# h stays in PSUM through h·cos(h): whole turns written as integers, no SBUF copy of h

## The chip, the cores and the metric

One Trainium2 chip, of which one core is used. The metric is device time in microseconds, the median of several executions. Of the kernel before three runs are known: 733.02, 732.50 and 732.21 us, median 732.5 us.

## The reference, cut to what matters

Attention over 2 batches of 8 heads and 768 positions gives `x`, 1536 tokens by 512. Two feed-forward parts follow. The change lies in the first of them:

```python
h = x @ w_in            # 1536x512 @ 512x2048
g = h * np.cos(h)
x = g @ w_out           # 2048x512
...
a = x @ w_a             # 512x1536
b = x @ w_b
return (a * b @ w_out2)
```

## The kernel before, in words

**Products.** Each float32 factor is split into a high part (rounded to the matrix engine's format `F32R`) and a low part (the rest), and a product takes three matmuls: high by high, high by low, low by high (lines 411 to 413, 473 to 475, 501 to 503). The 1536 tokens are three chunks `c` of 512. The first part's 2048 hidden columns are 16 blocks of 128, in groups of 4, 6 and 6. For a block and a chunk, `h_step` makes an `h` of 128x512 in PSUM with 12 matmuls, `h_mid` turns it into g, and `split_g` into the pair `gh` (ScalarE, line 455) and `gl` (GpSimd's subtraction, line 138). There are 48 such `h`, numbered 0 to 47 here in the order in which they are made. When all blocks of a group have their g for a chunk, `y_part` runs four partial products `y`, each of three matmuls for every block of the group, and VectorE adds them up in SBUF (lines 477, 479).

**Steps of h_mid.** ScalarE copies h/2π from PSUM into the SBUF tile `hs` (line 434). VectorE adds 0.25 and a large constant, which rounds to whole turns (line 435), then subtracts the constant and `hs` (line 436). ScalarE takes the sine (line 440), which by the shift of a quarter turn is the cosine of h. VectorE multiplies `hs` times 2π with it (line 443). Both `hs` and `u` have three buffers; a buffer of `u` is free again once GpSimd has made `gl` from it. Blocks 0 and 1 of the first chunk are made while the attention ends, by `early_turns` and `early_rest`, which call `h_turns`, `h_sin` and `h_mult` one by one; the other 46 go through `h_mid`.

**Weights.** A weight comes as a float64 in memory. Each of 68 blocks is converted: ScalarE takes an absolute value (line 351), VectorE runs four operations on whole numbers and bounds (lines 358 to 362), ScalarE rounds the high part (line 368), GpSimd subtracts for the low part (line 138). `fetch` writes these conversions between the products, up to 20 blocks ahead. The load of the next block waits on SyncE's queue until VectorE's last operation on the block two before has read its buffer.

**Buffers in PSUM.** In this part the tag `h` has four buffers of one bank, used in turn by `h` and, in the second part, by `a` and `b`; `y` and `o` have four more. A buffer of `h` is released by the last instruction that reads it.

**Order.** In the first and second feed-forward part only TensorE's instructions stand in the written order (`LATE_ORDER`). The orders on VectorE, ScalarE and GpSimd are made by a planner from modelled times when the kernel is built; on the chip each engine then runs its list strictly in that order. `in_turn` keeps the sines in the order in which they are written.

Of the kernel before, what the change touches and what calls it, by code (L numbers as in the profile page):

```python
# [10 lines left out]
F32 = mybir.dt.float32  # L11
# [3 lines left out]
I32 = mybir.dt.int32  # L15
AF = mybir.ActivationFunctionType
ALU = mybir.AluOpType
# [6 lines left out]
TWO_PI = 2.0 * math.pi  # L24
# [4 lines left out]
SC, TR = 2, 4  # L29
QP = (3, 13)  # L30
PTB = 3
# When each step of a tile's attention is due, in tiles from the tile's own; the steps are written in the order of these.
TABLE = {'S0': -0.894, 'T3': 0.134, 'TX': 1.203, 'TQ': -1.895, 'P0': 0.161, 'TK': -1.643, 'S1': -0.525, 'P1': 0.341, 'T0': -0.22, 'T1': -0.233, 'P2': 0.506, 'P3': 0.588, 'T2': -0.085, 'RL': 0.846, 'FIN': 0.963, 'L2': 0.298, 'B0': -0.757, 'B1': -0.676, 'L3': 0.443, 'XL': 1.457, 'B2': -0.371, 'B3': -0.219, 'KL': -1.201, 'L0': 0.036, 'L1': -0.108, 'H2': 0.02, 'H3': 0.339, 'XH': 1.381, 'E0': -0.666, 'E1': -0.347, 'QH': -1.59, 'KH': -1.325, 'E2': -0.243, 'H0': -0.146, 'H1': -0.218, 'E3': -0.066, 'SQ': -2.793, 'V': -0.869, 'PK': -0.368, 'QL': -1.371, 'FK': -1.121, 'VG': 1.106, 'LQ': -4.408, 'LK': -2.688, 'LV': -1.259}
BIAS = (-2.925, 0.022)
CONV = ((-0.4, 0.192), (0, 1.145), (2, 1), (11.427, 0.333))
# [12 lines left out]
def tile_kernel(ctx, tc, q, k, v, n_global, n_local, w_in, w_out, w_a, w_b, w_out2, out):  # L48
    nc = tc.nc
# [17 lines left out]
    mo = ctx.enter_context(tc.tile_pool(name="mo", bufs=2))  # L67
# [4 lines left out]
    def f(ap):  # L72
        return ap.bitcast(F32)
# [11 lines left out]
    ng, nl = counts[:, 0, 3:4], counts[:, 1, 3:4]  # L85

    def read_counts():
        """The two int64 scalars as floats: high word (one more where the low word reads as negative) times 2^32, plus the low word."""
        w = counts
        nc.vector.tensor_copy(out=w[:, :, 0:2], in_=words)  # L90
        nc.vector.tensor_scalar(out=w[:, :, 2:3], in0=w[:, :, 0:1], scalar1=0.0, scalar2=None, op0=ALU.is_lt)
        nc.vector.tensor_tensor(out=w[:, :, 2:3], in0=w[:, :, 2:3], in1=w[:, :, 1:2], op=ALU.add)
        nc.vector.scalar_tensor_tensor(out=w[:, :, 3:4], in0=w[:, :, 2:3], scalar=4294967296.0, in1=w[:, :, 0:1], op0=ALU.mult, op1=ALU.add)
# [19 lines left out]
    quarter = const.tile([P, 1], F32, tag="quarter", name="quarter")  # L113
# [33 lines left out]
    pinned = [True]  # L147

    def in_turn(x):
        """Keeps the functions that share no table of ScalarE in the order in which they are written."""  # L150
        if prev and pinned[0]:
            tc.add_manual_dep(x.ins, prev[0], mybir.DependencyInfo(mybir.DependencyClass.NoSync, mybir.DependencyReason.DATA),
                              reason="table order")
        prev[:] = [x.ins.name]
# [36 lines left out]
        nc.vector.tensor_tensor(out=kx[:, i % 2, 1, hps], in0=tk, in1=f(kx[:, i % 2, 0, hps]), op=ALU.subtract)  # L191

    def first_keys(i):
        """Keeps the first keys of a batch when its first tile has come."""
        if i % NQ == 0:
            pool_copy(kg, f(kx[:, i % 2, :, :, :GLOB]).rearrange("p a h s -> p (a h) s"))

    def put_first_keys(i):
        """After the scores of tile i, the first keys of the batch take the place of its own first ones."""
        if 0 < i % NQ < NQ - 1:  # L200
            pool_copy(kx[:, i % 2, :, :, :GLOB].rearrange("p a h s -> p (a h) s"), f(kg))

    def split_v(i):
        """Three bfloat16 parts of V, the first with a column of ones beside it for the sum of the weights."""
        b, t = divmod(i, NQ)
        vx = at.tile([P, H, 3 * D + 2], BF16, tag="vx", name=f"vx{i}", bufs=3)
        vn = nat.pop(i)["v"]
        nc.gpsimd.memset(vx[:, :, D:D + 2], 1.0)
        pool_copy(vx[:, :, 0:D], vn)
        pool_sub(vn, vn, vx[:, :, 0:D])  # L210
        pool_copy(vx[:, :, VP[1]], vn)
        pool_sub(vx[:, :, VP[2]], vn, vx[:, :, VP[1]])
        if t == 0:
            vg = at.tile([GLOB, H, 3 * D + 2], BF16, tag="vg", name=f"vg{i}", bufs=1)
            pool_copy(vg, vx[:GLOB])
            vg_of[b] = vg
        vx_of[i] = vx
# [77 lines left out]
        x_of[i] = xn  # L295

    def first_values(i):
        """After the products of tile i with V, the first values of the batch take the place of its own first ones."""
        if 0 < i % NQ < NQ - 1:
            nc.sync.dma_start(out=vx_of[i][:GLOB], in_=vg_of[i // NQ])  # L300

# [81 lines left out]
    now_conv = {}  # L383

    def conv_op(x):
        """The next of VectorE's four operations on block x."""
        if x not in now_conv:
            now_conv[x] = conv_ops(x)
        now_conv[x].pop(0)()
        if not now_conv[x]:  # L390
            del now_conv[x]
            done[1] += 1
# [38 lines left out]
    def h_turns(hps, shape, nm):  # L431
        hs = mo.tile(shape, F32, tag="hs", name="hs" + nm, bufs=3)
        u = mo.tile(shape, F32, tag="u", name="u" + nm, bufs=3)
        nc.scalar.activation(out=hs, in_=hps, func=AF.Copy, scale=1.0 / TWO_PI)  # L434
        nc.vector.tensor_scalar(out=u, in0=hs, scalar1=0.25, scalar2=MAGIC, op0=ALU.add, op1=ALU.add)  # L435
        nc.vector.scalar_tensor_tensor(out=u, in0=u, scalar=MAGIC, in1=hs, op0=ALU.subtract, op1=ALU.subtract)  # L436
        return hs, u

    def h_sin(hs, u):
        in_turn(nc.scalar.activation(out=u, in_=u, func=AF.Sin, bias=quarter, scale=-TWO_PI))  # L440

    def h_mult(hs, u):
        nc.vector.scalar_tensor_tensor(out=u, in0=hs, scalar=TWO_PI, in1=u, op0=ALU.mult, op1=ALU.mult)

    def h_mid(hps, shape, nm):
        x = h_turns(hps, shape, nm)
        h_sin(*x)
        h_mult(*x)
        return split_g(x[1], shape, nm)

    def split_g(u, shape, nm):
        pool, bufs = (post["mo"], NG[1]) if slot("g", *NG) else (mo, NG[0])
        gh = pool.tile(shape, F32R, tag="gh", name="gh" + nm, bufs=bufs)
        gl = pool.tile(shape, F32R, tag="gl", name="gl" + nm, bufs=bufs)
        nc.scalar.activation(out=gh, in_=u, func=AF.Copy)  # L455
        pool_sub(gl, u, f(gh))
        return gh, gl
# [114 lines left out]
            fn()  # L572

    def general_attention(ga, gps):
        """Any n_global and n_local: every key, with the masks worked out for each tile of queries."""
        xT_of.clear()
        half = S // 2
        for b in range(B):
# [10 lines left out]
            for t in range(NQ):  # L589
# [27 lines left out]
                for h in range(H):  # L617
# [5 lines left out]
                    for z in range(2):  # L623
# [3 lines left out]
                                                       op0=ALU.mult, op1=ALU.add)  # L627
# [18 lines left out]
                i = b * NQ + t  # L646
                c, u = divmod(i, TPC)
# [41 lines left out]
            nc.scalar.activation(out=d[:, 0, x], in_=d[:, 1, 1 - x], func=AF.Copy)  # L689

    def early_h(j, half):
        """A product of the second part while the attention's last steps are on their way."""
        if half == 0:
            early[0, j] = psum("h", [P, CH], f"h0_0_{j}")
        proj(early[0, j], ready[j], xT_of[0], range(2 * half, 2 * half + 2))
# [11 lines left out]
    other_i = const.tile([P, 1], I32, tag="otheri", name="other_i")  # L707

    def beyond():
        """Whether n_global and n_local go beyond what the tiles above hold."""  # L710
        nc.vector.tensor_scalar(out=other[:, 0:1], in0=nl, scalar1=1.0, scalar2=None, op0=ALU.is_lt)
        nc.vector.tensor_scalar(out=other[:, 1:2], in0=nl, scalar1=float(P - GLOB + 1), scalar2=None, op0=ALU.is_gt)
        nc.vector.tensor_scalar(out=other[:, 2:3], in0=ng, scalar1=float(GLOB), scalar2=None, op0=ALU.is_gt)
        nc.vector.tensor_tensor(out=other[:, 3:4], in0=other[:, 0:1], in1=other[:, 1:2], op=ALU.add)
        nc.vector.tensor_tensor(out=other[:, 3:4], in0=other[:, 3:4], in1=other[:, 2:3], op=ALU.add)
        nc.vector.tensor_copy(out=other_i, in_=other[:, 3:4])
# [3 lines left out]
    def boxed(x, fn):  # L720
# [4 lines left out]
    step = {  # L725
        "LQ": lambda i: i and load("q", i),
        "LK": lambda i: i and load("k", i),
        "LV": lambda i: load("v", i),
        "SQ": scale_q, "V": split_v,
        "TQ": boxed("Q", lambda i: turned("q", i)), "QH": lambda i: q_hi(i, box["Q", i]), "QL": lambda i: q_lo(i, box.pop(("Q", i))),  # L730
        "TK": boxed("K", lambda i: turned("k", i)), "KH": lambda i: k_hi(i, box["K", i]), "KL": lambda i: k_lo(i, box.pop(("K", i))),
        "FK": first_keys, "PK": put_first_keys, "RL": weights_sum, "FIN": finish, "VG": first_values,
        "TX": boxed("X", turn_x), "XH": lambda i: x_hi(i, box["X", i]), "XL": lambda i: x_lo(i, box.pop(("X", i)))}
    for quad in range(2):
        step[f"S{quad}"] = boxed(quad, lambda i, quad=quad: scores(i, quad))
        for a in range(2):
            x = 2 * quad + a
# [6 lines left out]
    parts = slice(0, HP // 2), slice(HP // 2, HP)  # L744
# [68 lines left out]
```

## Time and profile before

| what | value |
|---|---|
| median of three runs | 732.5 us |
| span of the profiled execution, first to last instruction | 731.0 us |
| around the span (median less span) | 1.5 us |
| PE busy / VectorE (DVE) busy / ScalarE (ACT) busy / GpSimd (POOL) busy | 676.8 / 510.7 / 303.3 / 289.8 us |
| mean granted TensorE clock | 0.967 of full speed |
| chain that ended last | PE 50%, DVE 35%, ACT 6% |

The page gives no time of its own for the profiled execution beside its span. Busy times are summed over the whole span; the attention takes about the first 119 us, the first feed-forward part lies between some 114 and 450 us, the second behind it. A row `a <- b` in the lists of waits reads: a sat idle until b had ended.

### The profile page before, as it was taken

To read this page: it belongs to the slowest core of one execution; us is meant where nothing else is said; L and a number is where in the kernel's file an instruction comes from. 1 tells how busy PE (TensorE), PEld (TensorE's weight loads), DVE (VectorE), ACT (ScalarE), POOL (GpSimd) and SP (SyncE) were. 2 spreads that over 40 slices of the span, in tenths; PEclk is the share of its full clock that TensorE was granted. 3 is DMA by queue.
4 is the path that set the end of the run, shared out by engine and by line. 5 is a ranking of instruction groups with operands and counts; after the bars stand their busy time and mean duration, and the time that the engine had idled before them with its cause. 6 is when DMAs were issued, how large, how long until landed. Compare 5 with 4: busy or idle time off the path is not lost.

```text
span 731.0 us, 10359 instructions
## 1 busy us (share of the span) xinstructions
PE 676.8 (93%) x3936; PEld 556.5 (76%) x3936; DVE 510.7 (70%) x901; ACT 303.3 (41%) x559; POOL 289.8 (40%) x263
## 2 busy tenths in 40 slices
PE   4899998799885999999989698999999999999996
PEld 3778887588763788788878486888888888888885
DVE  6999898999999979859979715885727322222223
ACT  4798886554445444444454413334314111111110
POOL 5789851664444434425252404435315211111110
PEclk9999999989987799999999799999999999999998
DMA  9944320223333202201303101333301000000004
GB/s 210 249 108 107 81 48 1 86 71 103 98 103 115 87 30 87 87 1 58 105 11 109 64 0 31 106 114 95 117 1 57 1 1 0 1 1 0 1 29 150
DMA packets 65084, 49.80 MB, mean 68 GB/s; under 512 B 39168, under 2 KB 59648, under 8 KB 65024
## 3 DMA queue, kind: packets, MB, share of 16 engines
q1 hardware_dynamic: 65024, 49.04, 23.4%
q8 instruction: 33, 0.54, 0.3%
q14 instruction: 27, 0.22, 0.1%
HBM read 45.09 MB, written 3.15 MB: 66 GB/s over the span
## 4 chain that ended last, share of the span: by engine, by line
PE 50%; DVE 35%; ACT 6%; issue 4%; POOL 2%; DMA 2%; SPq 0%; POOLq 0%; ACTq 0%; DVEq 0%
DVE cv L361 6%; DVE u L436 5%; PE o L502 4%; PE o L503 4%; PE o L501 4%; DVE cv L362 4%; PE b L413 4%; PE b L412 4%; PE b L411 4%; PE a L412 4%; PE a L411 4%; PE a L413 4%; DVE u L435 4%; DVE cv L358 3%; DVE cv L360 3%
## 5 line engine op out<-in xcount | busy, mean ns | idle before, releaser
L138 POOL TENSOR_TENSOR wl<-cv,wh 128x512 fp32r<-128x512 f32 x68 | 97.1, 1431 | 167.1 <-ACT wh L368 163.9
L138 POOL TENSOR_TENSOR glu<-as,ghu 128x512 fp32r<-128x512 f32 x36 | 47.5, 1320 | 158.5 <-ACT ghu L455 158.5
L491 DVE TENSOR_TENSOR as<-b,as 128x512 f32<-128x512 f32 x36 | 24.8, 689 | 117.6 <-PE b L413 116.4
L138 POOL TENSOR_TENSOR gl<-u,gh 128x512 fp32r<-128x512 f32 x48 | 69.8, 1464 | 74.4 <-ACT gh L455 62.3
L411 PE MATMUL h<-xTh,wh 128*128 128x512 f32 x192 | 79.1, 412 | 7.6 <-ACT hs L434 5.8
L473 PE MATMUL y<-gh,wh 128*128 128x512 f32 x192 | 75.4, 393 | 9.2 <-ACT gh L455 9.2
L474 PE MATMUL y<-gl,wh 128*128 128x512 f32 x192 | 76.0, 396 | 6.4 <-POOL gl L138 6.4
L412 PE MATMUL h<-xTl,wh 128*128 128x512 f32 x192 | 79.0, 411 | 0.0
L413 PE MATMUL h<-xTh,wl 128*128 128x512 f32 x192 | 78.6, 409 | 0.0
L475 PE MATMUL y<-gh,wl 128*128 128x512 f32 x192 | 75.2, 392 | 0.0
L368 ACT ACTIVATE wh<-cv 128x512 fp32r<-128x512 f32 x68 | 42.7, 628 | 69.1 <-DVE cv L362 58.2
L440 ACT ACTIVATE u<-u,quarter 128x512 f32<-128x512 f32 x48 | 34.7, 723 | 72.1 <-DVE u L436 72.1
L507 DVE TENSOR_TENSOR oacc<-o,oacc 128x512 f32<-128x512 f32 x60 | 41.2, 690 | 31.6 <-PE o L503 31.6
L411 PE MATMUL a<-yh,wh 128*128 128x512 f32 x144 | 57.2, 398 | 6.3 <-ACT as L488 4.2
L411 PE MATMUL b<-yh,wh 128*128 128x512 f32 x144 | 57.6, 400 | 3.0 <-ACT hs L434 3.0
L488 ACT ACTIVATE as<-a 128x512 f32<-128x512 f32 x36 | 21.4, 593 | 88.6 <-PE a L413 88.6
L361 DVE SCALAR_TENSOR_TENSOR cv<-raw,cv 128x512 int32<-128x512 int32 x62 | 57.4, 926 | 0.9
L412 PE MATMUL a<-yl,wh 128*128 128x512 f32 x144 | 57.1, 396 | 0.6 <-DVE yl L482 0.6
L413 PE MATMUL b<-yh,wl 128*128 128x512 f32 x144 | 57.4, 398 | 0.0
L412 PE MATMUL b<-yl,wh 128*128 128x512 f32 x144 | 57.2, 398 | 0.0
L413 PE MATMUL a<-yh,wl 128*128 128x512 f32 x144 | 57.0, 396 | 0.0
L351 ACT ACTIVATE cv<-raw 128x512 f32<-128x512 f32 x62 | 41.4, 668 | 37.2 <-POOL wl L138 18.0
(106 smaller groups left out, 1540.7 us busy)
## 6 DMA issues: line engine op xcount, KB each, us to landing
raw<-in_moe_w_out_dram SPq DMA_DIRECT2D x26, 512.0 KB, 3.3
raw<-in_moe_w_in_dram SPq DMA_DIRECT2D x12, 512.0 KB, 3.7
raw<-in_moe_w_a_dram SPq DMA_DIRECT2D x12, 512.0 KB, 3.6
raw<-in_moe_w_b_dram SPq DMA_DIRECT2D x12, 512.0 KB, 3.6
nv<-in_v_dram SPq DMA_DIRECT2D x12, 256.0 KB, 4.3
out_dram<-oacc SPq DMA_DIRECT2D x12, 256.0 KB, 2.9
nq<-in_q_dram SPq DMA_DIRECT2D x11, 256.0 KB, 3.6
nk<-in_k_dram SPq DMA_DIRECT2D x11, 256.0 KB, 4.4
```

The source lines that it names most:

```text
L138: nc.gpsimd.tensor_tensor(out=dst, in0=a, in1=b, op=ALU.subtract)
L351: nc.scalar.activation(out=f(c), in_=f(top), func=AF.Abs)
L361: lambda: nc.vector.scalar_tensor_tensor(out=c, in0=top, scalar=-0x40000000, in1=c, op0=ALU.bitwise_and, op1=ALU.bitwise_or),
L368: nc.scalar.activation(out=hi, in_=f(cvs[x]), func=AF.Copy)
L411: nc.tensor.matmul(dst, wh[:, kk, :], xh[:, kk, :], start=(kk == 0), stop=False)
L412: nc.tensor.matmul(dst, wh[:, kk, :], xl[:, kk, :], start=False, stop=False)
L413: nc.tensor.matmul(dst, wl[:, kk, :], xh[:, kk, :], start=False, stop=(kk == KD - 1))
L436: nc.vector.scalar_tensor_tensor(out=u, in0=u, scalar=MAGIC, in1=hs, op0=ALU.subtract, op1=ALU.subtract)
L473: nc.tensor.matmul(yps, wh[:, m, :], gh, start=(x == 0), stop=False)
L474: nc.tensor.matmul(yps, wh[:, m, :], gl, start=False, stop=False)
L475: nc.tensor.matmul(yps, wl[:, m, :], gh, start=False, stop=(x == len(items) - 1))
L507: nc.vector.tensor_tensor(out=acc[:, u, :], in0=ops, in1=acc[:, u, :], op=ALU.add)
```

## The change

`h_mid` no longer calls `h_turns`, `h_sin` and `h_mult`. ScalarE reads h in PSUM once and writes round(h/2π + 0.25) as a 32-bit integer into the tile that held `hs`. VectorE's next operation takes 2π times that integer off h, which it reads in PSUM. The sine's scale is 1 instead of -2π. VectorE multiplies h, again read in PSUM, with the sine. The two early blocks keep the old steps. Comments and docstrings were removed too; nothing else is different.

```diff
     def h_mid(hps, shape, nm):
-        x = h_turns(hps, shape, nm)
-        h_sin(*x)
-        h_mult(*x)
-        return split_g(x[1], shape, nm)
+
+        turns = mo.tile(shape, I32, tag="hs", name="ht" + nm, bufs=3)
+        u = mo.tile(shape, F32, tag="u", name="u" + nm, bufs=3)
+        nc.scalar.activation(out=turns, in_=hps, func=AF.Copy, bias=0.25, scale=1.0 / TWO_PI)
+        nc.vector.scalar_tensor_tensor(out=u, in0=turns, scalar=-TWO_PI, in1=hps, op0=ALU.mult, op1=ALU.add)
+        in_turn(nc.scalar.activation(out=u, in_=u, func=AF.Sin, bias=quarter, scale=1.0))
+        nc.vector.tensor_tensor(out=u, in0=hps, in1=u, op=ALU.mult)
+        return split_g(u, shape, nm)
```

## Rows read from the trace of the kernel before

**Rows 1.** The page's first part: busy us, share of the span, instructions.
```profile
PE 676.8 (93%) x3936; PEld 556.5 (76%) x3936; DVE 510.7 (70%) x901; ACT 303.3 (41%) x559; POOL 289.8 (40%) x263
```

**Rows 2.** Stretches: length, busy PE, PEld, DVE, ACT, POOL; TensorE clock, DMA share, GB/s.
```profile
121.40:237.00 115.60, 98.38 (x387) 77.95 (x387) 114.06 (x150) 57.80 (x96) 57.97 (x40) 0.90 0.29 91
237.00:404.00 167.00, 162.61 (x699) 133.16 (x700) 143.04 (x192) 76.72 (x130) 65.84 (x46) 0.97 0.20 64
404.00:420.00 16.00, 8.73 (x26) 6.36 (x25) 12.15 (x17) 7.78 (x14) 7.75 (x6) 0.78 0.20 67
...
457.00:731.00 274.00, 267.45 (x1180) 221.22 (x1178) 119.21 (x176) 60.42 (x99) 66.88 (x51) 0.99 0.14 45
```

**Rows 3.** TensorE's waits from 121.4 to 237 us: total us, times, longest.
```profile
PE h L411 <- ACT hs L434: 5.8, 2, 3.0
PE y L473 <- ACT gh L455: 4.5, 2, 3.4
PE y L474 <- POOL gl L138: 4.0, 3, 1.9
```

**Rows 4.** VectorE's groups from 121.4 to 237 us: count, busy us, mean ns.
```profile
L436 DVE SCALAR_TENSOR_TENSOR u<-u,hs 128x512 f32<-128x512 f32 x17 | 19.1, 1121 | 0.1
...
L443 DVE SCALAR_TENSOR_TENSOR u<-hs,u 128x512 f32<-128x512 f32 x18 | 15.4, 857 | 0.4 <-ACT u L440 0.4
...
L435 DVE TENSOR_SCALAR u<-hs 128x512 f32<-128x512 f32 x17 | 12.6, 740 | 0.0
```

**Rows 5.** GpSimd's subtractions for gl from 121.4 to 237 us.
```profile
L138 POOL TENSOR_TENSOR gl<-u,gh 128x512 fp32r<-128x512 f32 x17 | 25.9, 1523 | 18.8 <-ACT gh L455 10.3 <-issue 8.5
```

**Rows 6.** Single lines over the span: ns min/median/max, first and last start.
```profile
L435 DVE TENSOR_SCALAR u<-hs x48: 410/420/1522, 117.9 to 411.0; 128x512 f32<-128x512 f32 x48
...
L436 DVE SCALAR_TENSOR_TENSOR u<-u,hs x48: 677/693/1827, 118.3 to 413.8; 128x512 f32<-128x512 f32 x48
...
L443 DVE SCALAR_TENSOR_TENSOR u<-hs,u x48: 675/688/1776, 126.3 to 415.6; 128x512 f32<-128x512 f32 x48
...
L507 DVE TENSOR_TENSOR oacc<-o,oacc x60: 675/692/692, 508.7 to 724.5; 128x512 f32<-128x512 f32 x60
```

**Rows 7.** Instructions in order of time at 189 us: start us, length us.
```profile
188.82 0.68 DVE L477 COPY yacc<-y 128x512 f32<-128x512 f32 x1
188.93 0.72 ACT L440 ACTIVATE u<-u,quarter 128x512 f32<-128x512 f32 x1
189.04 1.30 POOL L138 TENSOR_TENSOR wl<-cv,wh 128x512 fp32r<-128x512 f32 x1 [2.23 <-ACT wh L368]
...
189.69 1.20 DVE L443 SCALAR_TENSOR_TENSOR u<-hs,u 128x512 f32<-128x512 f32 x1 [0.19 <-ACT u L440]
```

**Rows 8.** Two instructions in order of time at 215 to 222 us.
```profile
215.77 0.79 PE L411 MATMUL h<-xTh,wh 128*128 128x512 f32 x1 [2.97 <-ACT hs L434]
...
221.20 0.68 DVE L443 SCALAR_TENSOR_TENSOR u<-hs,u 128x512 f32<-128x512 f32 x1
```

**Rows 9.** TensorE's waits from 365 to 380 us.
```profile
PE y L473 <- ACT gh L455: 1.2, 1, 1.2
PE y L474 <- POOL gl L138: 0.9, 1, 0.9
```

**Rows 10.** Instructions in order of time where the second part begins.
```profile
408.07 0.58 ACT L434 ACTIVATE hs<-h 128x512 f32<-128x512 f32 x1
...
408.70 0.50 PE L411 MATMUL b<-yh,wh 128*128 128x512 f32 x1 [3.03 <-ACT hs L434]
...
410.97 1.50 DVE L435 TENSOR_SCALAR u<-hs 128x512 f32<-128x512 f32 x1
...
415.61 0.68 DVE L443 SCALAR_TENSOR_TENSOR u<-hs,u 128x512 f32<-128x512 f32 x1
...
417.55 0.79 PE L411 MATMUL a<-yh,wh 128*128 128x512 f32 x1 [4.24 <-ACT as L488]
```

**Rows 11.** The first wait of TensorE behind 237 us.
```profile
237.75 0.80 PE L473 MATMUL y<-gh,wh 128*128 128x512 f32 x1 [3.49 <-ACT gh L455]
```

## The prediction, made before the changed kernel was built
> **What bounds the kernel now.** I read the page's busy times first, then the stretches, then TensorE's waits, then VectorE's groups in the stretch where TensorE waits. Over the span TensorE is the busy engine (93%) and VectorE has 30% to spare [rows 1], but that is an average over stages. From 121.4 to 237 us, the first half of the first feed-forward part, VectorE works 114.06 of 115.60 us and TensorE 98.38, at 0.90 of its clock [rows 2]. At the rate of the last stretch (267.45 us for 1180 matmuls, 0.2267 us each) the 387 matmuls would take 87.7 us: 27.9 us are lost in this stretch, in waits and at the lower clock. From 237 to 404 us TensorE is busy 162.61 of 167 us and bounds; from 404 to 420 us it is busy 8.73 of 16 [rows 2].
>
> What TensorE waits for there is ScalarE's copy of h (5.8 us), gh (4.5 us) and gl (4.0 us) [rows 3]. ScalarE is busy only half of the stretch [rows 2]; its list stands behind VectorE's results. The stretch ends at 237.75 us, when gh of product 17 releases a wait of 3.49 us [rows 11]. That moment is set by VectorE's list, which has hardly a gap before it. So the stretch becomes shorter by what VectorE saves up to there.
>
> VectorE's operations on h take far more than they need: the medians of lines 435, 436 and 443 are 420, 693 and 688 ns, their longest 1522, 1827 and 1776 [rows 6], and in the stretch their means are 740, 1121 and 857 [rows 4]. The excess is GpSimd. At 189 us GpSimd's subtraction runs 1.30 us from 189.04; line 443, with both inputs in SBUF, starts at 189.69 and lasts until the subtraction has ended and its own time has passed, 1.20 us [rows 7]. Line 477, which reads PSUM, runs into the same subtraction and takes 0.68. Line 507, with one input in PSUM, never takes over 692 ns in 60 times [rows 6].
>
> **The change, part by part.** *VectorE's operations.* Of products 2 to 17, the 16 that end in the stretch by the new way, each loses 420 + 693 + 688 = 1801 ns undisturbed and gets two operations with one input in PSUM. I price these at line 507's 692 ns, 1384 together: 0.417 us saved. Line 507 adds two floats; a scalar_tensor_tensor with an integer input and PSUM is not in the trace. From below it is the 0.41 us of the shortest row on h, from above line 436's mean under GpSimd, 1.121 us [rows 4, 6]; line 507 is nearest, because where an input lies made the difference in rows 6, and the kind of operation did not (677 for line 436 and 675 for line 507 at the least).
>
> By the Trainium skill (VectorE: DVE Perf Modes, section on the TRN2 errata) an operation from PSUM pays 120 cycles beside its elements and one from SBUF 58, an estimate of 65 ns more for each new operation; 32 of them would take 2.1 us off the gain, and the time below would be 718.4. The trace disagrees: 692 ns from PSUM, 688 from SBUF [rows 6].
>
> *The blocking.* The excess over the medians is (740-420) + (1121-693) + (857-688) = 917 ns for each product. It does not all go: GpSimd's subtraction stays (1.52 us each [rows 5]), and when VectorE's next conversion operation comes up while it runs, that one waits. A blocked operation waits up to 1.13 us (1827-693); in that time one new operation of 0.69 is done, 61% of the wait. So I take 0.61 x 0.917 = 0.56 us; the bounds are 0 (all passed on to conversions) and 0.917 (none).
>
> *The sine between them.* The old list had other work between lines 436 and 443; even so line 443 waited 0.19 us for the sine (0.72 us) in rows 7, and 0.4 us in all [rows 4]. With less work to fill in I take 0.10 us for each product, an estimate between none and the 0.19.
>
> Sum: 0.417 + 0.56 - 0.10 = 0.88 us, x 16 = 14.1 us, all on the path. TensorE's floor (27.9 us) is not reached. Later products save as much, but from 237 to 404 us TensorE bounds, and there it counts only where TensorE waits: gh and gl of a chunk's last product cost 1.2 + 0.9 = 2.1 us at 375 us [rows 9]. Lines 435 and 436 stand in that chain, with up to 1.5 and 1.8 us under GpSimd; one operation of 0.69 takes their place, so I count these 2.1 us as gone.
>
> *ScalarE* writes integers where it wrote floats: at least line 434's 0.58 [rows 10], at most the sine's 0.72 [rows 7], so 0.14 x 16 = 2.2 us, hidden by its idle half [rows 2]. If that cover were gone, the sine would start so much later.
>
> *The longer hold in PSUM.* An h was released by the copy; now it is released by the multiplication. TensorE waited for the copy of product 15 until 215.77; line 443 of it ends at 221.88 [rows 8], 6.1 us later. TensorE will wait longer for h there, but the h that it has ahead are enough for VectorE: what ends the stretch is gh of product 17, which needs VectorE's list and no new h beyond those already made. I cost it at nothing in this stretch. Behind the waiting matmul stand the y, which wait for gh and gl anyhow.
>
> At the start of the second part it shows. There b takes the buffer of the last h and starts at 408.70 [rows 10]. Now it needs the last multiplication. Line 435, which had waited for a buffer of `u`, starts at 410.97; from there 0.69 + 0.72 + 0.69 gives 413.1. The b took until 413.31 (417.55 less the wait of 4.24), 4.6 us, so it would end at 417.7, against 417.55 when the next a started. 0.1 us, which I drop. If the multiplication stayed at 416.29, b would end at 420.9: 3.4 us lost.
>
> *Loads.* SyncE's loads of weights follow VectorE's conversions and come earlier with them; the DMA engines are busy 0.29 of the stretch [rows 2], so nothing is added.
>
> The profiled span, 731.0, less 14.1 and 2.1 is 714.8; with the 1.5 us by which the median lies above the span, **716.3 us**, in a range of its own from 709 to 723.
>
> **The rivals.** *A, the wait is passed on.* VectorE's list is in order; if a conversion operation stands behind every new one, it meets the rest of GpSimd's subtraction. For: the operations on h are only 19.1 + 15.4 + 12.6 of VectorE's 114.06 us in the stretch [rows 2, 4]; most of what stands behind them is conversions. Against: one new operation of 0.69 us is done meanwhile in any case. Only 0.417 - 0.10 = 0.32 x 16 = 5.1 us and the 2.1 stay: 725.3. The Trainium skill (SBUF — State Buffer, section Who interferes with whom) states the lock behind it: an operation of VectorE with two SBUF inputs and one of GpSimd that reads SBUF shut each other out for the whole instruction. The trace agrees, 1827 ns at most for 693 [rows 6].
>
> *B, all the blocking goes*, because the two new operations happen to stand where GpSimd runs. GpSimd's gl starts just behind ScalarE's gh of the same product, when the next product's operations are due. (0.417 + 0.917) x 16 = 21.3 and 2.1: 709.1. TensorE's floor, 27.9 in the place of 21.3, sets the end of this case at 702.5.
>
> *C, slower: the hold in PSUM decides.* TensorE waited twice for a copy of h in the stretch [rows 3]; each wait grows by 6.1 us [rows 8], 12.2 together. The waits for gh and gl behind them, 4.5 + 4.0, are shortened by as much as VectorE does not move, which leaves 3.7, and the start of the second part adds its 3.4: 739.6 if VectorE gains nothing. It decides if VectorE's gain is under 7.1 us, 0.44 us for each product, so if the new operation on integers is blocked by GpSimd like line 436. For: VectorE was nearly always at the end of the chain, and four buffers are few. Against: line 507.
>
> *D, it does nothing to the time.* The planner makes the lists anew and puts the saved time into conversions that are due later, so that gh of product 17 comes when it came: 732.5. Against: conversions are bound to run no more than 20 blocks ahead.
>
> **How the numbers follow.** The forecast has 0.52, A 0.17, B 0.14, C 0.10, D 0.07. The range from 703 to 731 us holds the forecast, A, nearly all of B and the better part of D's spread; it leaves out C, the rest of D and little above or below. About 0.2%, 1.5 us, is what a measurement tells from no change. Faster by more: forecast, A and B, 0.83. Within: most of D, 0.06. Slower: C and the rest, 0.11.
>
> **What would show it.** Two operations of VectorE in h_mid with a longest time near 0.69 us, however GpSimd runs; if the one on integers reaches 1.5, C's condition is met. The means of conversion lines 358 to 362 in the stretch: unchanged for the forecast, higher for A, lower for B. TensorE's waits for h named on VectorE's multiplication instead of ScalarE's copy, and the gh that ended the stretch some 14 us earlier. From there to 404 us TensorE as busy as now. A wait of b at the start of the second part of over 7 us that is not made up behind would make the forecast wrong, and so would VectorE still full up to 237 us.

## The result, and the profile after

| | before | after |
|---|---|---|
| median | 732.76 us | 707.35 us (705.98 to 708.92) |
| ratio, 95% interval | | 0.9645 [0.9626, 0.9664] |
| span of the profiled execution | 731.0 us | 706.5 us |
| mean granted TensorE clock | 0.967 | 0.987 |

The forecast was 716.3 us in a range from 703 to 731. The sign came as forecast, and in the first stretch the mechanism too; the gain was 25.4 us where 16.2 had been worked out, and 8.3 us of it came at a place that had been put at nothing.

Line numbers moved: the whole turns are line 449 (ScalarE), the subtraction of the turns 450, the sine 451, the multiplication 452, gh 459; the y matmuls 477 to 479, the first copy of y 481, its additions 483, `as` 492. The page's first part after, against [rows 1]:

```profile
PE 667.0 (94%) x3936; PEld 550.3 (78%) x3936; DVE 467.9 (66%) x855; ACT 302.3 (43%) x559; POOL 281.9 (40%) x263
```

VectorE lost 46 instructions and 42.8 us of work. The stretches of after, with the columns of [rows 2]. The first begins where line 435 of the second early product starts in either kernel (121.39 us before, 122.50 after; the change's first instruction comes behind that). The second is the part in which TensorE bounds:

```profile
122.50:228.50 106.00, 94.36 (x387) 74.78 (x387) 103.02 (x134) 57.49 (x97) 53.55 (x40) 0.95 0.31 95
237.00:404.00 167.00, 165.20 (x722) 136.29 (x721) 115.36 (x167) 80.51 (x137) 68.35 (x51) 0.99 0.21 66
```

The 387 matmuls that took 115.6 us take 106.0 now; VectorE still works nearly all the time there. TensorE's waits of after from 117 to 460 us (what waited <- for what: total us, times, longest), against [rows 3, 9 to 11]:

```profile
PE h L411 <- DVE u L452: 8.9, 5, 3.6
PE y L478 <- POOL gl L138: 2.6, 3, 1.2
...
PE b L411 <- DVE u L452: 1.8, 1, 1.8
PE y L477 <- ACT gh L459: 1.4, 2, 1.1
```

The waits for h and for b are named on VectorE's multiplication, as predicted, and those for gh and gl have shrunk from 8.5 us in the stretch alone to 4.0 in all.

VectorE's two new operations over the span of after (ns min/median/max, first and last start), against [rows 6]:

```profile
L450 DVE SCALAR_TENSOR_TENSOR u<-ht,h x46: 671/677/689, 128.6 to 390.0; 128x512 f32<-128x512 int32 x46
```
```profile
L452 DVE TENSOR_TENSOR u<-h,u x46: 673/683/693, 133.4 to 393.2; 128x512 f32<-128x512 f32 x46
```

None of the 92 was stretched, where the operations they replaced reached 1.5 to 1.8 us. VectorE's groups of after in the first stretch (count, busy us, mean ns, idle before), against [rows 4]:

```profile
L361 DVE SCALAR_TENSOR_TENSOR cv<-raw,cv 128x512 int32<-128x512 int32 x20 | 21.3, 1063 | 0.5
L360 DVE TENSOR_SCALAR cv<-cv 128x512 int32<-128x512 int32 x21 | 20.2, 960 | 0.6
L362 DVE SCALAR_TENSOR_TENSOR cv<-raw,cv 128x512 int32<-128x512 int32 x20 | 17.8, 888 | 0.2
L358 DVE TENSOR_SCALAR cv<-cv 128x512 f32<-128x512 f32 x22 | 15.5, 706 | 1.1 <-ACT cv L351 0.7
L452 DVE TENSOR_TENSOR u<-h,u 128x512 f32<-128x512 f32 x16 | 10.9, 682 | 0.6 <-ACT u L451 0.6
L450 DVE SCALAR_TENSOR_TENSOR u<-ht,h 128x512 f32<-128x512 int32 x16 | 10.8, 676 | 0.0
```

And the conversion groups of before in its stretch from 121.4 to 237 us:

```profile
L361 DVE SCALAR_TENSOR_TENSOR cv<-raw,cv 128x512 int32<-128x512 int32 x20 | 20.4, 1018 | 0.3
...
L362 DVE SCALAR_TENSOR_TENSOR cv<-raw,cv 128x512 int32<-128x512 int32 x20 | 17.5, 874 | 0.1
...
L360 DVE TENSOR_SCALAR cv<-cv 128x512 int32<-128x512 int32 x21 | 15.0, 716 | 0.3
L358 DVE TENSOR_SCALAR cv<-cv 128x512 f32<-128x512 f32 x22 | 14.1, 641 | 0.4 <-ACT cv L351 0.2
```

The conversions became dearer, 74.8 us where they took 67.0, above all line 360. Experiment 12 shows that GpSimd is what makes them dear; that they now meet the subtractions which the operations on h no longer meet is my reading of it.

**Where the time came from.** I set the starts of the same matmuls against each other. Product 22 starts at 249.80 us before and 239.61 after: 10.2 us come from the first stretch. Another 0.7 comes near 308 us (gl) and 2.7 near 375 us (gh and gl, [rows 9]), so the second part starts 13.6 us earlier. Its first 72 matmuls (three a and three b) take 28.4 us in before and 20.1 in after: 8.3 us. Then 1.6 us at 450 us before, and about 1 us at the end. The first of the 72 matmuls in before, behind the last matmul of the y ahead of it (start us, length us, engine, line):

```profile
397.12 0.39 PE L475 MATMUL y<-gh,wl 128*128 128x512 f32 x1
397.34 0.39 PE L411 MATMUL a<-yh,wh 128*128 128x512 f32 x1
```

and the same in after, with the one wait among the 72:

```profile
383.55 0.39 PE L479 MATMUL y<-gh,wl 128*128 128x512 f32 x1
383.77 0.39 PE L411 MATMUL a<-yh,wh 128*128 128x512 f32 x1
...
393.90 0.50 PE L411 MATMUL b<-yh,wh 128*128 128x512 f32 x1 [1.80 <-DVE u L452]
```

The y behind them starts at 425.70 us in before and at 403.83 in after. TensorE waited 3.03 and 4.24 us in between in before [rows 10], and 1.80 in after.

### The profile page after: what moved, and what is told of

The parts are those of the page before. It is cut to its first block, busy times and chain, and to the rows that moved or that the text cites. A ratio compares the mean times of both kernels' runs of the same rounds, so it can differ in the third digit from the quotient of the medians.

```text
span 706.5 us, 10307 instructions
## 1 busy us (share of the span) xinstructions
PE 667.0 (94%) x3936; PEld 550.3 (78%) x3936; DVE 467.9 (66%) x855; ACT 302.3 (43%) x559; POOL 281.9 (40%) x263
## 4 chain that ended last, share of the span: by engine, by line
PE 70%; DVE 20%; ACT 4%; issue 2%; DMA 2%; POOL 2%; SPq 0%; POOLq 0%; ACTq 0%
PE o L506 5%; PE o L507 5%; PE o L505 5%; PE b L411 5%; PE b L413 5%; PE b L412 5%; PE a L412 4%; PE a L413 4%; PE a L411 4%; PE y L478 4%; PE y L479 4%; PE y L477 4%; DVE cv L361 4%; PE h L413 4%; PE h L412 4%; PE h L411 4%
## 5 line engine op out<-in xcount | busy, mean ns | idle before, releaser
L138 POOL TENSOR_TENSOR wl<-cv,wh 128x512 fp32r<-128x512 f32 x68 | 92.1, 1359 | 191.3 <-ACT wh L368 185.9
L495 DVE TENSOR_TENSOR as<-b,as 128x512 f32<-128x512 f32 x36 | 24.8, 688 | 113.4 <-PE b L413 112.3
L411 PE MATMUL h<-xTh,wh 128*128 128x512 f32 x192 | 77.5, 404 | 10.8 <-DVE u L452 8.9
L138 POOL TENSOR_TENSOR gl<-u,gh 128x512 fp32r<-128x512 f32 x48 | 67.6, 1418 | 35.6 <-ACT gh L459 31.6
L412 PE MATMUL h<-xTl,wh 128*128 128x512 f32 x192 | 77.2, 402 | 0.0
L413 PE MATMUL h<-xTh,wl 128*128 128x512 f32 x192 | 77.1, 401 | 0.0
L358 DVE TENSOR_SCALAR cv<-cv 128x512 f32<-128x512 f32 x68 | 46.6, 686 | 24.8 <-ACT cv L351 24.2
L492 ACT ACTIVATE as<-a 128x512 f32<-128x512 f32 x36 | 21.3, 593 | 86.9 <-PE a L413 86.9
```

Source lines behind the costliest of these rows:

```text
L138: nc.gpsimd.tensor_tensor(out=dst, in0=a, in1=b, op=ALU.subtract)
L358: lambda: nc.vector.tensor_scalar(out=f(c), in0=f(c), scalar1=word_const(896 << 20), scalar2=word_const((1151 << 20) - 1), op0=ALU.max, op ...
L411: nc.tensor.matmul(dst, wh[:, kk, :], xh[:, kk, :], start=(kk == 0), stop=False)
L412: nc.tensor.matmul(dst, wh[:, kk, :], xl[:, kk, :], start=False, stop=False)
L413: nc.tensor.matmul(dst, wl[:, kk, :], xh[:, kk, :], start=False, stop=(kk == KD - 1))
```

## The experiments

Theories: **blocking** (the gain is VectorE's: one operation fewer, and two that GpSimd can't shut out), **backlog** (the same saving works a second time where the second part begins, because VectorE's list is late there), **hold** (the longer hold in PSUM costs time that something else must make up), and **one cure is enough** (whatever takes the blocking away does as well). All are timed against the kernel before in the same session.

**1 and 2. The new steps in half of the products.** In the first kernel products 2 to 29 have them, in the second (with `< 2`) products 30 to 47.

```diff
     def h_mid(hps, shape, nm):
+        if int(nm.split('_')[1]) == 2:
+            x = h_turns(hps, shape, nm)
+            h_sin(*x)
+            h_mult(*x)
+            return split_g(x[1], shape, nm)
```

> The new steps only for the first two groups of blocks (products 2 to 29); the last group (30 to 47) has the old steps. Theory 'backlog': of the 24.5 us that the changed kernel's span is shorter, TensorE's timeline shows some 11 us won before product 22 and some 13 us behind product 32 (0.7 at 308 us, 2.7 at 375 us, 8.3 at the start of the second part, 1.6 of clock behind it), because VectorE no longer runs up to 7 us behind TensorE there. So this kernel keeps the first part and loses the second: 732.8 - 11 = 720 to 723 us. Rival 'per product': the gain comes evenly from each product: 18 of 46 are lost, 707.4 + 10 = 717. Rival 'planner': the later gain came from a lucky order of the lists and not from the last group's steps: about 708 to 712.

> The new steps only for the last group (products 30 to 47), the old ones before. Theory 'backlog': the stretch to 237 us stays as in the kernel before, the places at 375 us, at the start of the second part and behind it are won: 732.8 - 13 = 718 to 722 us. Rival 'per product': 18 of 46 of the gain, 732.8 - 10 = 723. Rival 'planner': no more than 2 or 3 us won, about 730.

Measured: 719.14 us (0.9812 [0.9795, 0.9828]) and 720.61 us (0.9839 [0.9822, 0.9855]). By their spans the first gains 13.2 us, the second 12.3, together 25.5 against the 24.5 of the whole change (by the medians 13.2 and 11.7, against 25.4). The first starts product 22 11.8 us before the kernel before does, the second only 0.4. The first 72 matmuls of the second part take 28.4 us in before and 20.1 in after; they take 25.6 in the first kernel, whose last steps are old, and 18.5 in the second. The two halves of the gain come in different places and nearly add up, and of the second half I had costed only the 2.1 us at 375 us. The first kernel came out 0.9 us under my 720 to 723, on the side of the 717 of an even gain per product. The trace of after speaks against that rival: it starts product 22 and product 32 (301.48 us before, 291.29 after) earlier by the same 10.2 us, so ten products with the new steps won nothing. A wait of the first kernel shows what it is:

```profile
PE a L411 <- ACT as L496: 5.8, 1, 5.8
```

That wait ends at 405.25 us, in the place of the 4.24 us of before [rows 10]: `as` comes late behind VectorE's additions and multiplications. With new steps there (second kernel) no a waits for `as`.

**3. The copy of h kept, the count not.** ScalarE writes a copy of h, and both VectorE operations read it in place of PSUM: two operations as in after, two SBUF inputs as in before.

```diff
+        hc = post["mo"].tile(shape, F32, tag="hc", name="hc" + nm, bufs=3)
+        nc.scalar.activation(out=hc, in_=hps, func=AF.Copy)
-        ... scalar_tensor_tensor(out=u, in0=turns, ..., in1=hps, ...)
+        ... scalar_tensor_tensor(out=u, in0=turns, ..., in1=hc, ...)
-        nc.vector.tensor_tensor(out=u, in0=hps, in1=u, op=ALU.mult)
+        nc.vector.tensor_tensor(out=u, in0=hc, in1=u, op=ALU.mult)
```

> As the changed kernel, but ScalarE also copies h to SBUF (one more ScalarE instruction of 0.58 us for each product), and both of VectorE's operations read that copy; PSUM is free again after the copies. Theory 'blocking': two inputs in SBUF are shut out by GpSimd again, means of about 1.0 to 1.1 us for the first and 0.85 for the multiplication in the stretch instead of 0.68; about 0.4 us of each product and part of the gain at the start of the second part is lost: 714 to 721 us. Rival 'count': it is the operation fewer that counts, and reading PSUM nothing: 706 to 709. Rival 'hold': the shorter hold in PSUM gives back waits of TensorE for h (8.9 us in 5 waits in the changed kernel): under 706.

Measured: 721.54 us (0.9834 [0.9811, 0.9858]). The two operations over its span (ns min/median/max):

```profile
L452 DVE SCALAR_TENSOR_TENSOR u<-ht,hc x46: 676/685/1778, 135.0 to 402.1; 128x512 f32<-128x512 int32 x46
```
```profile
L454 DVE TENSOR_TENSOR u<-hc,u x46: 676/686/1781, 136.8 to 404.7; 128x512 f32<-128x512 f32 x46
```

The medians are those of after (677 and 683), the longest those of before. The time lies 0.5 us over my 714 to 721. So 14.2 of the 25.4 us hang on the input in PSUM. The copy also stands in front of the first operation, which could be a delay of its own; but VectorE waited 7.0 us for the copy over the whole span, and 7.8 us for the integers in after.

**4. The same copy, read by nobody.** It separates the price of ScalarE's extra operation from the blocking.

```diff
+        hc = post["mo"].tile(shape, F32, tag="hc", name="hc" + nm, bufs=3)
+        nc.scalar.activation(out=hc, in_=hps, func=AF.Copy)
```

> The changed kernel with ScalarE's additional copy of h to SBUF for each product, which nothing reads: VectorE reads PSUM as in the changed kernel. It tells apart what made the kernel with the copy in SBUF 14 us slower than the changed one. Theory 'blocking': VectorE's operations stay at 0.68 us and only ScalarE has 46 x 0.58 us more, which its idle half takes: 706 to 710 us. Rival 'ScalarE': the additional instruction delays the sines and gh, and that was the 14 us: 718 to 722.

Measured: 706.23 us (0.9645 [0.9627, 0.9663]), as after. ScalarE's 46 extra operations cost nothing, so, with those 7.0 and 7.8 us, the loss in 3 is the blocking.

**5. Only the multiplication from PSUM.** The kernel before, with one line changed: three operations, the copy kept, h held until the multiplication.

```diff
-        h_mult(*x)
+        nc.vector.tensor_tensor(out=x[1], in0=hps, in1=x[1], op=ALU.mult)
```

> The kernel before with one edit: the multiplication reads h in PSUM (a product of two tensors) instead of the SBUF copy times 2 pi; copy, rounding and subtraction stay as they were. The hold in PSUM is as long as in the changed kernel. Theory 'blocking': of the 917 ns of blocking for each product only the multiplication's 169 ns can go, half of them passed on, and no operation is saved: 728 to 733 us. Rival 'hold': what the longer hold costs stands alone here: 735 to 740. Rival 'count': nothing, 732.8.

Measured: 730.07 us (0.9965 [0.9951, 0.9979]). Its waits from 117 to 460 us:

```profile
PE h L411 <- DVE u L448: 10.8, 6, 5.2
PE b L411 <- DVE u L448: 7.4, 1, 7.4
```

The hold shows itself at full size, a wait of 7.4 us for b included, and the next a, which waited 4.24 us in [rows 10], waits no longer for `as`, and only 1.4 us for a multiplication. The median is 2.3 us under that of before, so the 735 to 740 of the hold theory fall. The trace says less: the execution that it shows took 733.03 us, where the other four took 729.92 to 730.63, its span of 731.2 us is that of before, and TensorE's waits from 117 to 460 us sum to 36.2 us against 33.1. The hold mostly moved waits from one place to another; where the 2.3 us came from is not shown.

**6 to 8. What is left after the change.** A fifth buffer for h (and three for y), the first copy of a y on ScalarE, and both.

```diff
-            return post["ps"].tile(shape, F32, tag=kind, name=nm, bufs=4)
+            return post["ps"].tile(shape, F32, tag=kind, name=nm, bufs={"h": 5, "y": 3}[kind])
```
```diff
-            nc.vector.tensor_copy(out=acc[:, m, :], in_=yps)
+            nc.scalar.activation(out=acc[:, m, :], in_=yps, func=AF.Copy)
```

> The changed kernel with five buffers in PSUM for h, a and b and three for y and o (it has four and four). Theory 'blocking': TensorE's 8.9 us of waits for the multiplication to release h move to other places, since VectorE's list sets when the stretch ends: 705 to 709 us. Rival 'hold': the waits for h go and the time with them: 699 to 704. Rival 'three are too few for y': 710 or more.

> The changed kernel with the 12 first copies of y from PSUM (line 481, 0.68 us each, all in the stretch that VectorE bounds) moved from VectorE to ScalarE. Theory: VectorE still sets the end of the stretch, so 12 x 0.60 = 7.2 us less work comes out there, less about half where such a copy ran beside a blocked GpSimd subtraction and the wait is passed on: 3.5 to 7 us won, 700 to 704. Rival 'VectorE no longer bounds': 706 to 709. Rival 'ScalarE's list': the copies wait for TensorE in ScalarE's list and delay sines behind them: over 709.

> Both of the last two edits on the changed kernel. Theory 'blocking': as the kernel with the first y on ScalarE alone, within 2 us: 699 to 704. Rival 'hold': with less work on VectorE the release of h is the next thing late, and the fifth buffer wins some 3 us more: 695 to 699.

Measured: 706.96 us (0.9659 [0.964, 0.9679]), 707.27 (0.9646 [0.963, 0.9662]) and 704.79 (0.9619 [0.9603, 0.9635]). With five buffers the waits for h are gone, and these stand in their place:

```profile
PE y L477 <- DVE yacc L481: 5.3, 3, 2.8
PE y L477 <- ACT gh L459: 4.9, 3, 1.7
PE y L478 <- POOL gl L138: 4.0, 3, 2.1
```

So a wait for h was mostly VectorE's lateness under another name. The fifth buffer was taken from y, though, and the 5.3 us in front of y may be the price of that; the two were not tried apart. The ScalarE copy was a miss: I had expected 700 to 704. In its stretch from 122.5 to 228.5 us VectorE has the 8.2 us of the copies less to do, and stands idle 7.2 us in front of line 358, where it stood 1.1 in after:

```profile
L358 DVE TENSOR_SCALAR cv<-cv 128x512 f32<-128x512 f32 x22 | 18.0, 819 | 7.2 <-ACT cv L351 7.1
```

It waits for the absolute value of the next weight block, on ScalarE; what makes that late was not tried. With the two edits together 2.6 us are won; 704.79 lies just over my 699 to 704.

**9 and 10. GpSimd's subtraction for gl on VectorE**, in `h_mid` alone; the tenth kernel adds the edits of 8.

```diff
-        pool_sub(gl, u, f(gh))
+        nc.vector.tensor_tensor(out=gl, in0=u, in1=f(gh), op=ALU.subtract)
```

> The changed kernel with the subtraction that makes gl of the first part done by VectorE (two inputs in SBUF) instead of GpSimd. In the changed kernel's stretch from 122.5 to 228.5 us the four conversion lines of VectorE take 29 us more than their undisturbed lengths, for 40 subtractions of GpSimd, 0.73 us each; 17 of these are gl. Theory 'blocking': the means of the conversion lines fall (together from 3.6 to about 2.9 us), some 12 us of waiting go and 17 x 0.60 = 10 us of work come: within some us of the changed kernel, 702 to 710. Rival 'the excess is no lock': the conversions stay at 3.6 us and VectorE has 10 us more to do where it bounds: 714 to 720.

> The same on top of the kernel with the first y on ScalarE and five buffers for h (704.8 us). Theory 'blocking': the two shares nearly cancel again, 701 to 708 us. Rival as above: 711 to 716.

Measured: 691.17 us (0.9437 [0.9414, 0.9459]) and 693.23 us (0.9473 [0.9452, 0.9495]): a second miss, this time by 11 us to the good of my 702 to 710 (and by 8 of 701 to 708). The edits of 8 then win nothing: they lose some 2 us, with the runs of the two kernels touching at 692.85 us. VectorE's groups of the ninth kernel from 122.5 to 228.5 us:

```profile
L361 DVE SCALAR_TENSOR_TENSOR cv<-raw,cv 128x512 int32<-128x512 int32 x21 | 17.4, 831 | 0.1
L360 DVE TENSOR_SCALAR cv<-cv 128x512 int32<-128x512 int32 x22 | 16.4, 743 | 0.2
...
L461 DVE TENSOR_TENSOR gl<-u,gh 128x512 fp32r<-128x512 f32 x18 | 12.2, 680 | 0.0
```

VectorE takes on 12.2 us of gl and has back 14.3 on its conversions (each group's count times the fall of its mean; the four means fall from 3.62 to 2.95 us, as I had expected). That alone is 2 us. Product 17's multiplication, though, ends at 213.3 us in place of 227.7. Two conversions stand behind it that stood ahead of it (2 x 2.95), VectorE is idle 1.4 us less, and some 5 us I can't assign: the shorter way from gh to gl and the new order were not tried apart.

**11. Is one cure enough?** The kernel before with that edit alone: three operations on SBUF, but no gl on GpSimd.

> The kernel before, with its old steps and the copy of h in SBUF, but gl of the first part subtracted by VectorE as in the kernel that ran in 691.2 us. It asks whether reading PSUM is still worth its 25 us when GpSimd has only the weights' subtractions left in this part. Theory 'blocking': half of GpSimd's work is gone and with it about half of the blocking of lines 435, 436 and 443 (0.92 us for each product), so this kernel gains much from it, as the changed one did: 712 to 722 us, and the change is worth 21 to 31 us beside it. Rival 'one cure is enough': the blocking is gone either way and only the one operation fewer is left between the two: 696 to 704.

Measured: 701.99 us (0.9589 [0.9573, 0.9605]): a miss for my price of blocking, and inside the rival's 696 to 704, though not for the rival's reason alone, since line 436 is still blocked. Its groups from 121.4 to 237 us, of VectorE and then of GpSimd:

```profile
L436 DVE SCALAR_TENSOR_TENSOR u<-u,hs 128x512 f32<-128x512 f32 x20 | 18.0, 898 | 0.0
L443 DVE SCALAR_TENSOR_TENSOR u<-hs,u 128x512 f32<-128x512 f32 x21 | 15.9, 755 | 0.0
```
```profile
L138 POOL TENSOR_TENSOR wl<-cv,wh 128x512 fp32r<-128x512 f32 x23 | 46.0, 2003 | 81.6 <-ACT wh L368 81.5
```

Without gl on GpSimd the change is worth 10.8 us (701.99 to 691.17), not 25.4: much of its gain is the cure of one ill that can be cured otherwise. How much is not settled by this: as in experiment 9, the planner put two conversions behind product 17's multiplication that stood ahead of it before (2 x 2.57 us by the means of this stretch), and this order was not tried by itself. What is left of GpSimd's work is itself stretched here, 2003 ns a piece against 1325 in the stretch of after: shutting out goes both ways.

**12. No subtraction on GpSimd in the first part**: the ninth kernel, and the weights' low parts on VectorE too.

```diff
+        if post:
+            nc.vector.tensor_tensor(out=lo, in0=f(cvs.pop(x)), in1=f(hi), op=ALU.subtract)
+        else:
             pool_sub(lo, f(cvs.pop(x)), f(hi))
```

> The changed kernel with gl of the first part and, from the end of the attention on, the low parts of the weights too subtracted by VectorE; GpSimd keeps glu of the second part alone. In the first part no instruction of GpSimd is left that could block VectorE. Theory 'blocking': the four conversion lines fall to their undisturbed 2.2 us together (2.95 with gl alone moved), which takes off about as much (0.74 us for each block) as the additional subtraction adds (0.60): 687 to 694 us, near the 691.2 of gl alone. Rival 'VectorE is overloaded': it has 0.6 us for each block more and the stretch grows by 10 us or more: 699 to 706.

Measured: **685.65 us** (0.9364 [0.9349, 0.938]), the fastest of all, 21.7 us below after and 1.4 under my 687 to 694. From 121.4 to 237 us, its engines and then four of VectorE's groups:

```profile
121.40:237.00 115.60, 113.36 (x492) 93.17 (x492) 112.27 (x204) 74.10 (x122) 3.98 (x3) 0.99 0.32 101
```
```profile
L361 DVE SCALAR_TENSOR_TENSOR cv<-raw,cv 128x512 int32<-128x512 int32 x22 | 15.1, 685 | 0.0
L362 DVE SCALAR_TENSOR_TENSOR cv<-raw,cv 128x512 int32<-128x512 int32 x22 | 15.1, 685 | 0.0
...
L358 DVE TENSOR_SCALAR cv<-cv 128x512 f32<-128x512 f32 x24 | 10.6, 444 | 0.8 <-ACT cv L351 0.7
L360 DVE TENSOR_SCALAR cv<-cv 128x512 int32<-128x512 int32 x24 | 10.0, 421 | 0.0
```

VectorE does 204 instructions in 112.3 us where before it did 150 in 114.1, and TensorE 492 matmuls where it did 387. The four conversion steps cost 2.24 us together, against 3.25 in before and 3.62 in after: this is what they cost undisturbed.

## Why the prediction was right, and where it was off

**VectorE bounds the first stretch: right.** Product 17's multiplication ended the list 115.6 us after line 435's start at 121.39 and now 105.2 after the one at 122.50, and TensorE's product 22 moved with it.

**The two operations at line 507's price: right.** 676 + 682 = 1358 ns for the 1384 taken; 92 of 92 below 0.70 us. By the Trainium skill (VectorE: DVE Perf Modes, section on the TRN2 errata) they should have paid an estimated 62 cycles (120 less 58) more than operations on SBUF; the rows still disagree, 677 and 683 ns from PSUM against 685 and 686 for the same two operations from SBUF in experiment 3.

**The blocking: right in kind, too hopeful in size.** It is what experiment 3 lost and 4 did not. The Trainium skill (SBUF — State Buffer, section Who interferes with whom) has the rule, that GpSimd, while it reads SBUF, shuts out operations of VectorE with two SBUF inputs; the trace agrees, 1778 ns against 689 at most for one operation with its input moved. But of the 0.917 us for each product I took 39% as passed on to the conversions. They rose by 74.8 - 67.0 = 7.8 us, and 16 x 0.917 is 14.7: 53%. The sign that I had set for the forecast, unchanged means of the conversions, failed with it (together 3.25 to 3.62 us, the sign of A), and it had never fitted my own 39%. Nor did most of this rise need the input in PSUM: in the first stretch of experiment 3 (122.5 to 235 us), where both operations are blocked again (means of 954 and 751 ns, 5.3 us over the medians in 16 products), the conversions take 73.4 us, nearly what they take in after.

**The sum of the stretch: 14.1 predicted, 9.9 to 11.3 found.** For the 16 products the operations on h took 47.1 us [rows 4] less 4.6 for the early products, 42.5, and take 21.7: 20.8 saved (21.3 in the prediction's terms, count and blocking). From that go 7.8 passed on (5.7), idle time 2.98 - 1.54 = 1.4 (1.6, as the wait for the sine), and one term that I had not: successive instructions of VectorE overlap in the trace by some 0.07 us (124.3 us of durations in 114.06 us of busy time before, 111.5 in 103.02 after), so that an instruction less saves less than its duration; 1.7 us less overlap in all, 1.1 of it for the 16 instructions that are gone. 20.8 - 7.8 - 1.4 - 1.7 = 9.9 us for VectorE. TensorE's product 22 came 10.2 us earlier, 11.3 counted from line 435's start.

**The rivals.** The share passed on, 53%, lies between the forecast's 39% and A's whole. B's number, 709.1, is the nearest to the time, but its sign, lower conversion means, did not come. D falls, since the same conversions stand ahead of product 17's multiplication in either list and it still came 9.3 us earlier.

**375 us: right.** 2.7 us against 2.1; the two waits are gone.

**The start of the second part: the step that failed.** "0.1 us, which I drop" was 8.3 us. I let line 435 start where it had started, at 410.97 us, and asked only what b would then wait for. But that start was itself the end of a late list: the last y ahead of the second part ended at 397.5 us, and VectorE added it up at 415.01, 17.5 us later. This backlog had grown in a stretch where TensorE bounds: for the y that ended at 322.7 us the addition had come 0.04 us later. Nothing in my stretch from 237 to 404 us, where TensorE bounds, charged for that lateness, and VectorE's saving there (143.04 us of work [rows 2] against 115.36) was put down as worthless. It shortened the backlog: in after the same y ends at 383.9, and its addition comes 9.8 us later. The same y is added up 14.6 us after its end in experiment 1, whose last steps are old, and 9.9 in experiment 2, whose last steps are new. Its addition in before:

```profile
415.01 0.68 DVE L479 TENSOR_TENSOR yacc<-y,yacc 128x512 f32<-128x512 f32 x1
```

and VectorE's list of after at that place:

```profile
390.05 0.68 DVE L450 SCALAR_TENSOR_TENSOR u<-ht,h 128x512 f32<-128x512 int32 x1
390.64 0.92 DVE L360 TENSOR_SCALAR cv<-cv 128x512 int32<-128x512 int32 x1
391.60 1.65 DVE L361 SCALAR_TENSOR_TENSOR cv<-raw,cv 128x512 int32<-128x512 int32 x1
393.17 0.68 DVE L452 TENSOR_TENSOR u<-h,u 128x512 f32<-128x512 f32 x1
393.77 0.68 DVE L483 TENSOR_TENSOR yacc<-y,yacc 128x512 f32<-128x512 f32 x1
```

The b waits 1.80 us for line 452, and by the time it has run, y and `as` are there. Of the 8.3 us, 7.27 - 1.80 = 5.5 are waits; the other 2.8 are matmuls that ran at the lower clock behind them (0.78 granted from 404 to 420 us of before [rows 2]). Experiments 1 and 2 show it from both sides: with old steps at this place the 72 matmuls take 25.6 us, with new ones 18.5.

**The hold: nothing seen of a cost.** TensorE waits 8.9 us for h in after, against 5.8 in before, and not 12.2 more; experiment 5 lost no time by it, and 6, which takes these waits away, won none. Rival C's condition, line 450 blocked, did not come.

**ScalarE and the loads: right.** 46 further operations on ScalarE changed nothing (experiment 4).

**Not foreseen:** 1.6 us at 450 us. Both kernels wait 2.02 us for yh and 0.64 for yl there, and then the granted clock differs, between the two levels in before (columns of [rows 2]):

```profile
450.00:457.00 7.00, 4.67 (x13) 3.47 (x14) 4.65 (x8) 2.93 (x5) 2.62 (x3) 0.77 0.30 83
```

and at the full 2.4 GHz in after:

```profile
430.00:437.00 7.00, 6.35 (x28) 5.01 (x28) 4.61 (x9) 2.94 (x5) 2.84 (x3) 1.00 0.53 150
```

The cause was not tried. The forecast was right in sign and range: a stretch 3 to 4 us too large, 8.3 us left out, and some 3 us in smaller places that I had not in the sum. That the time lies in the range is partly luck: 707.35 is below the 709 to 723 that I had given to the forecast alone, and the range down to 703 stood there for rival B, whose reason did not come.

## What to carry to other kernels

An engine that does not bound a stretch can still carry a backlog out of it: before a saving is priced at nothing, look how long after its input each result comes, and where that lateness is called in. Where VectorE and GpSimd both work on SBUF, a VectorE operation that reads one input from PSUM is not shut out, but of the blocking that this change took off the operations on h half (53%) came back on their neighbours; taking the work off GpSimd cured all of them, and here VectorE had the time for it (685.65 us). A wait named on a buffer may be the late engine under another name: a fifth buffer, taken from y, moved 8.9 us of waits and won nothing.

## What the runs showed of the hardware

ScalarE writes 32-bit integers from PSUM at the price of floats. Line 449 of after, in ns, against 0.58 us of line 434 in [rows 10]:

```profile
L449 ACT ACTIVATE ht<-h x46: 573/580/598, 126.9 to 387.1; 128x512 int32<-128x512 f32 x46
```

A scalar_tensor_tensor with an integer and a PSUM input takes 677 ns, no more than one on two floats in SBUF. And the subtraction of GpSimd over the span of experiment 11 went from 1267 ns to 5302 where VectorE's list left it no gap: it starts at 226.77 us, VectorE works without idle time until 230.92, and it ends 1.15 us behind that (GpSimd's spans are rough in the trace):

```profile
L138 POOL TENSOR_TENSOR wl<-cv,wh x68: 1267/1340/5302, 20.1 to 535.2; 128x512 fp32r<-128x512 f32 x68
```
